# Refitted engine orders, other mask forms and half-bank sums in a top-k attention and MLP-mixer kernel

## The chip, the cores and the metric

The kernel runs on one core of a Trainium2 chip. A core has a matrix engine (TensorE, PE), a vector engine (VectorE, DVE), an activation engine (ScalarE, ACT), a general engine (GpSimd, POOL) and queues that start transfers (SyncE, SP, among them). All run side by side, each takes its own instructions in order, and semaphores join them. The metric is device time in microseconds of one execution, as the median of several; the profile is of one execution.

## The reference

There are 8 batches of 8 heads, 576 rows and 64 columns per head. Each row of scores keeps its 32 largest, and the masked softmax weights the values; then an MLP mixer works on each batch, over the rows (256 hidden) and then over the 512 channels (1536 hidden).

```python
scores = scale * np.matmul(q, k.transpose(0, 1, 3, 2))
kth = np.partition(scores, -32, axis=-1)[..., -32:-31]
scores = np.where(scores >= kth, scores, -1000000000.0)
scores = scores - np.max(scores, axis=-1, keepdims=True)
attn = np.exp(scores); attn = attn / (np.sum(attn, axis=-1, keepdims=True) + 1e-09)
x = np.matmul(attn, v)            # then (B, S, H * D), as x of the mixer
h = np.maximum(x.transpose(0, 2, 1) @ w_tok1, 0.0) @ w_tok2
u = x + h.transpose(0, 2, 1)
out = u + np.maximum(u @ w_ch1, 0.0) @ w_ch2
```

## The kernel before

The kernel is straight-line code, written out by a planner. Each operation is added with its engine, an assumed duration, a due time, the operations it depends on and the buffers it takes and frees. The planner then walks a model of the engines: on each engine, of the operations that could start at the same time, the one with the earliest due time goes first. The result is only an order of instructions for each engine; on the chip they run as semaphores let them. The due times come from the table `W`, in units of `T` after a row's own time, so `W` sets priorities.

```python
W = dict(
    T=2.45, ev=-0.8, evh=0.45, seg=2.15, t2=3.1, ct=1.2, xm=3.65, dm=3.2, m5=3.25, ex=3.95, tn=3.15,
    z=6.0, mk=0.8, pm=3.85, rw=4.55, og=6.55, eg=2.8, ea=1.95, st=4.25, tr=0.35, pv=7.65, fin=8.2,
    mlp=15.75, stp=1.95, mlq=13.3, stq=0.85, hp=7.35, hps=1.55,
)
FORMS = ("DRDAD", "RDADA", "DRDRD", "RDDRA")   # 5 units of a pair of heads; pair p takes FORMS[p % 4]
LAST = ("DRRDR", "QAADA")                      # the last two of the 32 pairs
```

Two heads of a batch form a pair. A pair has five units: four full ones (128 query rows of both heads, so two rows of 128 x 576 scores) and a short one (64 remaining query rows of both heads, in one row). Every unit first goes the same way (shortened):

```python
om  # PE   L413/L405: scores into PSUM ("big": 4 buffers of two banks each)
evs # ACT  L471: copy of the scores to SBUF (S), one per row
# per row:
segs # DVE L478: 8 largest of each of 7 segments of the row
a1..a5 # DVE L481, L482, L489: from these, an upper threshold (thi)
cts # ACT  L492: Sign against the threshold, with a count (sg, cnt)
xm  # POOL L495: X = S * sg, once per unit
dm  # DVE  L503: 9 filler values that fix the rank
m   # DVE  L507: the 8 largest of X; the last is the exact threshold (tlo)
```

Then the masked exponential Pm is made in one of four forms, by the unit's letter:

```python
if form == "D":
    ex   # ACT  L515: E = exp(S)
    tn, zs, mk  # POOL L517, L520, L523: M = 0/1 mask from S and the threshold
    last # POOL L526: Pm = E * M
elif form in ("R", "Q"):
    if form == "R":
        ws # ACT L533: W = relu(tlo - S), one per row
    else:
        tn, zs, ws # POOL L517/540, L542, L546: W = min(S - tlo, 0), scaled
    og   # PE L553 and L413/L405: sink * W into PSUM, then the scores added on top once more
    last # ACT L559: Pm = exp(PSUM), one per row
else:    # "A"
    ex   # ACT L564: exp(S) into PSUM, one per row
    last # DVE L567: Pm = (S >= tlo) * exp, one per row
```

A transposing transfer turns Pm (the last two units of the last pair: PE and a DVE copy, L578 and L582), PE multiplies by the values (L436), and DVE divides by the row sums (L454, L455). After four pairs the mixer of that batch is spread among the next pairs' units; the last batch has nothing to hide behind and has a way of its own. Three of its four column blocks come early, and their part of the hidden sums is put aside in SBUF. When the last block is there, each of the 12 hidden blocks is finished so:

```python
for fc in range(NF):
    pb = Buf("big")
    o = plan.add("PE", 0.28, d, lambda ...: hidden(pb, fc, (NC - 1,)), ...)        # L736, two matmuls of 288 columns
    a = plan.add("DVE", 0.7, d + 0.3, lambda ...: nc.vector.tensor_tensor(         # L784
        out=part(fc), in0=row(pb.t), in1=part(fc), op=ALU.add), [o, ready[fc]], use=[pb, B_])
    relus.append(plan.add("ACT", 0.53, d + 0.6, lambda ...: nc.scalar.activation(  # L786
        out=H2.t[:, fc, :], in_=part(fc), func=AF.Relu), [a], use=[B_, H2]))
    if fc < NF - 2:
        # L768: five output sums of this hidden block, in three "big" buffers that stay taken
        prev = plan.add("PE", 1.09, d + 1.5, f, [relus[-1], prev], use=[H2] + outs)
```

So one "big" buffer of four is left for the sums of this loop.

Of the kernel before, what the change touches and what calls it, by code (L numbers as in the profile page):

```python
# [8 lines left out]
P = 128  # L9
# [7 lines left out]
SINK2 = float(2.0**50)  # L17

W = dict(
    T=2.45, ev=-0.8, evh=0.45, seg=2.15, t2=3.1, ct=1.2, xm=3.65, dm=3.2, m5=3.25, ex=3.95, tn=3.15,  # L20
    z=6.0, mk=0.8, pm=3.85, rw=4.55, og=6.55, eg=2.8, ea=1.95, st=4.25, tr=0.35, pv=7.65, fin=8.2,
    mlp=15.75, stp=1.95, mlq=13.3, stq=0.85, hp=7.35, hps=1.55,
)

FORMS = ("DRDAD", "RDADA", "DRDRD", "RDDRA")

LAST = ("DRRDR", "QAADA")
NEG = -float(2.0**120)
BIG = float(2.0**60)

# [178 lines left out]
def kernel(  # L209
# [11 lines left out]
    nc = tc.nc  # L221
# [3 lines left out]
    AF = mybir.ActivationFunctionType  # L225
# [27 lines left out]
    plan = Plan()  # L253
# [85 lines left out]
    def row(t):  # L339
        return flat(t)[:, L0 : L0 + S]  # L340

    def pair_ops(p):
# [76 lines left out]
        for g in range(5):  # L419
            n = 2 if g < 4 else 1  # L420
            bs, Ss = [Buf("big") for _ in range(n)], Buf("S")
            i0 = 9 * p + 2 * g
            om = plan.add("PE", 1.2 if g < 4 else 1.1, T * i0, lambda g=g, bs=bs: scores(g, bs, True), [eq, ek], acq=bs + [Ss], use=[qT, kT])
            PT.append(unit_ops(i0, n, bs, Ss, om, p, g, scores, [qT, kT]))


# [39 lines left out]
    def unit_ops(i0, n, s, S_, om, p, g, scores, qkT):  # L466
# [7 lines left out]
        for h in range(n):  # L474
# [17 lines left out]
            cts.append(plan.add("ACT", 0.77, th + W["ct"] * T, lambda h=h, i=i, r=r: nc.scalar.activation(  # L492
                out=sg.t[:, h, :], in_=S_.t[:, h, :], func=AF.Sign, scale=-CUT, bias=thi[:, r + 7 : r + 8],
                accum_out=cnt[:, i : i + 1]), [a5], acq=[sg] if h == 0 else [], use=[S_, sg]))
        xm = plan.add("POOL", 0.1 + 1.16 * n, te + W["xm"] * T, lambda: nc.gpsimd.tensor_tensor(  # L495
            out=X.t[:, XW - S : XW - S + n * S].rearrange("p (h c) -> p h c", h=n), in0=S_.t[:, 0:n, :], in1=sg.t[:, 0:n, :], op=ALU.mult),
            cts, acq=[X], use=[S_, sg])
        if not first_x:
# [14 lines left out]
        if form == "D":  # L513
            E, M, Z, nt = Buf("E"), Buf("M"), Buf("Z"), Buf("nt")
            ex = plan.add("ACT", 0.1 + 0.48 * n, te + W["ex"] * T, lambda: nc.scalar.activation(  # L515
                out=E.t[:, 0:n, :], in_=S_.t[:, 0:n, :], func=AF.Exp, scale=scale / UP), evs, acq=[E], use=[S_])
            tn = plan.add("POOL", 0.2, te + W["tn"] * T, lambda: nc.gpsimd.tensor_scalar(  # L517
                out=nt.t[:, 0:n], in0=tlo[:, r0 - n + 1 : r0 + 1], scalar1=-(1.0 - 2.0**-24), scalar2=0.0,
                op0=ALU.mult, op1=ALU.add), ms, acq=[nt])
            zs = [plan.add("POOL", 0.835, te + W["z"] * T + 0.01 * h, lambda h=h: nc.gpsimd.tensor_scalar(  # L520
# [8 lines left out]
        elif form in ("R", "Q"):  # L529

            Wm, es = Buf("M"), [Buf("big") for _ in range(n)]
            if form == "R":
                ws = [plan.add("ACT", 0.68, te + W["rw"] * T + 0.2 * h, lambda h=h: nc.scalar.activation(  # L533
                    out=Wm.t[:, h, :], in_=S_.t[:, h, :], func=AF.Relu, scale=-1.0,
                    bias=tlo[:, r0 - h : r0 - h + 1]), [ms[h]], acq=[Wm] if h == 0 else [], use=[S_, Wm])
                    for h in range(n)]
            else:
                nt, Z = Buf("nt"), Buf("Z")
                tn = plan.add("POOL", 0.2, te + W["tn"] * T, lambda: nc.gpsimd.tensor_scalar(
                    out=nt.t[:, 0:n], in0=tlo[:, r0 - n + 1 : r0 + 1], scalar1=-(1.0 - 2.0**-24), scalar2=0.0,  # L540
                    op0=ALU.mult, op1=ALU.add), ms, acq=[nt])
                zs = [plan.add("POOL", 0.835, te + W["z"] * T + 0.01 * h, lambda h=h: nc.gpsimd.tensor_scalar(  # L542
                    out=Z.t[:, h, :], in0=S_.t[:, h, :], scalar1=nt.t[:, n - 1 - h : n - h],
                    scalar2=16.0, op0=ALU.add, op1=ALU.mult), [tn], acq=[Z] if h == 0 else [],
                    use=[S_, nt, Z]) for h in range(n)]
                ws = [plan.add("POOL", 0.27 + 0.48 * n, te + W["mk"] * T, lambda: nc.gpsimd.tensor_scalar(  # L546
                    out=Wm.t[:, 0:n, :], in0=Z.t[:, 0:n, :], scalar1=0.0, scalar2=-float(2.0**40), op0=ALU.min,
                    op1=ALU.max), zs, acq=[Wm], use=[Z])]

            def again():  # L550
                for h in range(n):
                    for lo, hi in ((0, HS), (HS, S)):
                        nc.tensor.matmul(  # L553
                            out=row(es[h].t)[:, lo:hi], lhsT=sink[:, "RQ".index(form), :], rhs=Wm.t[:, h, lo:hi],
                            start=True, stop=False)
                scores(g, es, False)

            og = plan.add("PE", (1.2 if n == 2 else 1.1) + 0.3 * n, te + W["og"] * T, again, ws, acq=es, use=[Wm] + qkT)
            last = [plan.add("ACT", 0.535, te + W["eg"] * T + 0.2 * h, lambda h=h: nc.scalar.activation(  # L559
                out=Pm.t[:, h, 0:S], in_=row(es[h].t), func=AF.Exp, scale=scale / UP),  # L560
                [og], acq=[Pm] if h == 0 else [], use=[es[h], Pm]) for h in range(n)]
# [31 lines left out]
    def form_of(p, g):  # L593
        if p >= NPAIR - 2:
            return LAST[p - NPAIR + 2][g]
        return FORMS[p % len(FORMS)][g]

    def mlp_ops(b):
        X = xb[b]
# [62 lines left out]
        for fc in range(NF):  # L662
# [7 lines left out]
                            rhs=UT.t[:, cc, lo:hi], start=(cc == 0), stop=(cc == NC - 1))  # L670

            d = due()
            o = plan.add("PE", 1.02, d, f, uts + l3, acq=[pb] + ([H2] if fc == 0 else []), use=[UT, H2])
            h2.append(plan.add("ACT", 0.535, d + 1, lambda fc=fc, pb=pb: nc.scalar.activation(  # L674
                out=H2.t[:, fc, :], in_=row(pb.t), func=AF.Relu), [o], use=[pb, H2]))
        for s0 in (0, 2, 4):
# [5 lines left out]
            for h in range(sn):  # L682
                pb = Buf("one")
                for part in range(2):
                    def f(part=part, sc=s0 + h, pb=pb, r=r):
# [5 lines left out]
                        if part:  # L691
                            for cc in range(NC):
# [2 lines left out]
                                    start=False, stop=(cc == NC - 1))  # L695

                    d = due()
                    o = plan.add("PE", 1.6 if part else 1.33, d, f, dep + l4,
                                 acq=[] if part else [pb], use=[H2, pb] + ([UT] if part else []))
                    dep = [o]  # L700
                es.append(plan.add("ACT", 0.48, d + 1, lambda pb=pb, ob=ob, r=r, h=h: nc.scalar.copy(
# [11 lines left out]
    def mlp_tail(b, base, UT, H2, uts):  # L713
# [16 lines left out]
                return flat(B_.t).bitcast(f32)  # L730
            return B_.t[:, :, :, :].rearrange("p t h d -> p (t h d)")[:, 0:S]

        def hidden(pb, fc, ccs):
            for lo, hi in ((0, HS), (HS, S)):
                for cc in ccs:
                    nc.tensor.matmul(  # L736
                        out=row(pb.t)[:, lo:hi], lhsT=wc1b[:, cc, fc * P : (fc + 1) * P],
                        rhs=UT.t[:, cc, lo:hi], start=(cc == ccs[0]), stop=(cc == ccs[-1]))

        ready = []  # L740
        for fc in range(NF):
# [1 line left out]
            B_, half = parts[fc]  # L743
            d = base - T * W["hp"] + W["hps"] * T * fc
            dep = uts[0 : NC - 1] + l3 + (late_d if B_.tag in ("E", "Z") else [])
            o = plan.add("PE", 0.78, d, lambda fc=fc, pb=pb: hidden(pb, fc, range(NC - 1)), dep,
                         acq=[pb] + ([H2] if fc == 0 else []) + ([B_] if half == 0 else []), use=[UT, H2, B_])
            ready.append(plan.add("ACT", 0.525, d + 0.1, lambda fc=fc, pb=pb: nc.scalar.copy(
                out=part(fc), in_=row(pb.t)), [o], use=[pb, B_, H2]))
# [24 lines left out]
        relus = []  # L774
        prev = None
        for fc in range(NF):
            pb = Buf("big")
            B_, half = parts[fc]
            d += 1.4
            o = plan.add("PE", 0.28, d, lambda fc=fc, pb=pb: hidden(pb, fc, (NC - 1,)), uts + [ready[fc]],  # L780
                         acq=[pb], use=[UT, H2])
            if fc == 0:
                prev = plan.add("PE", 0.4, d + 0.1, lambda: residual((NC - 1,)), uts + [r1], use=[UT] + outs)
            a = plan.add("DVE", 0.7, d + 0.3, lambda fc=fc, pb=pb: nc.vector.tensor_tensor(  # L784
                out=part(fc), in0=row(pb.t), in1=part(fc), op=ALU.add), [o, ready[fc]], use=[pb, B_])
# [269 lines left out]
```

## Time and profile before

| what | value |
|---|---|
| time, median of three | 857.64 us (857.32 to 860.5) |
| span of the profiled execution | 858.9 us |
| instructions | 19498 |
| mean granted TensorE clock | 0.92 |
| HBM read, written | 35.85 MB, 9.44 MB |
| score matmuls L413 | 1400, 250.0 us busy |
| POOL product X L495 | 160, 344.7 us busy |
| DVE segment maxima L478 | 2016, 403.4 us busy |

The profile gives for every engine the time in which at least one of its instructions was running. Instructions of one engine overlap a little, so durations of single ones add up to more than the busy time of their group. PE is TensorE's matmul, PEld its weight load. A group line names the kernel's line, the engine, the operation, what it writes and reads, how often it ran, its busy time, the mean duration in ns, and the idle time of the engine just before it with what ended it. The clock is the share of TensorE's full rate that was granted in a stretch.

### The profile page before, as it was taken

How to read it: one execution, taken by the hardware profiler on the slowest of the kernel's cores; microseconds unless marked ns; L12 is line 12 of the kernel's file. 1: busy time of each engine (PE TensorE's matmuls, PEld its weight loads, DVE VectorE, ACT ScalarE, POOL GpSimd, SP SyncE). 2: the span in 40 equal slices, each digit the busy share in tenths (PEclk: the TensorE clock that was granted, in tenths of full speed). 3: DMA queues.
4: the chain of work that ended last, by engine and by line, in shares of the span. 5: the costliest groups of instructions: out<-in, count | busy, mean ns of one | idle time of the engine just before them, and what ended most of it. 6: DMA issues, size and time to landing. Idle time of an engine off the chain costs nothing.

```text
span 858.9 us, 19498 instructions
## 1 busy us (share of the span) xinstructions
PE 698.7 (81%) x5458; PEld 445.9 (52%) x5495; DVE 795.4 (93%) x4783; ACT 766.4 (89%) x1465; POOL 723.4 (84%) x557
## 2 busy tenths in 40 slices
PE   6756648898788898899688886888888886899984
PEld 4434425655456555565356554564555554575641
DVE  5999899998999999999999999999999999999852
ACT  6997778998999989999999999999899999999742
POOL 2999988899889998899998998899898999889600
PEclk9675688998999899999899998999899998999998
DMA  5985866436555446446565355746557345343401
GB/s 125 152 160 95 123 119 115 100 65 119 125 100 112 86 115 136 82 100 120 124 121 106 76 123 109 124 84 124 115 109 129 70 109 128 67 71 67 105 2 60
DMA packets 311061, 89.58 MB, mean 104 GB/s; under 512 B 303776, under 2 KB 305696, under 8 KB 310944
## 3 DMA queue, kind: packets, MB, share of 16 engines
q1 hardware_dynamic: 306992, 84.19, 49.8%
q0 software_dynamic: 2752, 3.77, 3.2%
q8 instruction: 45, 0.74, 0.4%
q14 instruction: 72, 0.59, 0.2%
q10 hardware_dynamic: 1200, 0.30, 0.2%
HBM read 35.85 MB, written 9.44 MB: 53 GB/s over the span
## 4 chain that ended last, share of the span: by engine, by line
DVE 42%; ACT 23%; PE 20%; issue 6%; POOL 5%; DMA 3%; SPq 1%; ACTq 0%; DVEq 0%; POOLq 0%
DVE cd L478 15%; DVE tlo L507 11%; ACT sg L492 8%; PE big L413 6%; PE big L688 6%; ACT S L471 5%; DVE cd L482 5%; DVE Pm L567 3%; DVE m L481 3%; ACT M L533 2%; ACT Pm L559 2%; POOL X L495 2%; DVE thi L489 2%; DVE X L503 2%; PE big L768 2%
## 5 line engine op out<-in xcount | busy, mean ns | idle before, releaser
L478 DVE MAX8 cd<-S 128x8 f32<-128x82 f32 (+1 forms) x2016 | 403.4, 230 | 18.0 <-ACT S L471 17.9
L495 POOL TENSOR_TENSOR X<-S,sg 128x1152 f32<-128x1152 f32 (+1 forms) x160 | 344.7, 2167 | 51.4 <-ACT sg L492 42.0
L413 PE MATMUL big<-kT,qT 64*128 64x288 f32 x1400 | 250.0, 478 | 45.5 <-ACT kT L394 31.8
L492 ACT ACTIVATE sg<-S,thi 128x576 bf16<-128x576 f32 x288 | 227.1, 790 | 13.2 <-POOL X L495 4.8
L507 DVE MAX8 tlo<-X 128x8 f32<-128x588 f32 x288 | 220.4, 765 | 3.0 <-POOL X L495 1.6
L413 PEld LDWEIGHTS big<-kT,qT 64*128 64x128 f32 x1400 | 151.6, 214 | 106.6 <-ACT kT L394 34.5
L471 ACT COPY S<-big 128x576 f32<-128x576 f32 x288 | 174.5, 651 | 9.3 <-PE big L413 8.8
L526 POOL TENSOR_TENSOR Pm<-E,M 128x1152 bf16<-128x1152 bf16 (+1 forms) x78 | 168.3, 2157 | 6.5
L520 POOL TENSOR_SCALAR Z<-S,nt 128x576 f32<-128x576 f32 x141 | 105.0, 745 | 13.5
L688 PE MATMUL big<-wc2b,H 128*128 128x512 bf16 (+1 forms) x401 | 99.7, 387 | 13.2 <-ACT S L471 5.9
L668 PE MATMUL big<-UT,wc1b 128*128 128x288 bf16 x672 | 91.2, 286 | 13.7 <-ACT H L674 5.4
L481 DVE MAX8 m<-cd 128x8 f32<-128x14 f32 (+1 forms) x576 | 97.4, 170 | 0.3
L482 DVE MATCH_REPLACE8 cd<-m,cd 128x14 f32<-128x14 f32 (+1 forms) x576 | 97.4, 169 | 0.0
L523 POOL TENSOR_SCALAR M<-Z 128x1152 bf16<-128x1152 f32 (+1 forms) x78 | 82.2, 1054 | 6.8
L515 ACT ACTIVATE E<-S 128x1152 bf16<-128x1152 f32 (+1 forms) x78 | 84.7, 1086 | 2.7 <-POOL Pm L526 0.8
L668 PEld LDWEIGHTS <-wc1b 128*128 128x128 bf16 x672 | 64.1, 97 | 40.0 <-issue 23.5
L553 PE MATMUL big<-M,sink 128*128 128x288 bf16 x190 | 39.4, 313 | 43.6 <-ACT M L533 27.8
L688 PEld LDWEIGHTS <-H 128*128 128x128 bf16 (+1 forms) x420 | 40.6, 101 | 61.7 <-issue 24.9
L559 ACT ACTIVATE Pm<-big 128x576 bf16<-128x576 f32 x95 | 56.7, 654 | 16.9 <-PE big L413 16.9
L533 ACT ACTIVATE M<-S,tlo 128x576 bf16<-128x576 f32 x93 | 69.7, 783 | 2.2 <-DVE tlo L507 2.0
L436 PEld LDWEIGHTS <-PT 128*128 128x128 bf16 x1600 | 54.9, 100 | 15.2 <-issue 7.1
L436 PE MATMUL big<-vb,PT 128*128 128x65 bf16 x1600 | 57.1, 197 | 5.8 <-DMA PT<-Pm 5.1
(109 smaller groups left out, 914.3 us busy)
## 6 DMA issues: line engine op xcount, KB each, us to landing
qL<-in_q_dram SPq DMA_DIRECT2D x64, 128.0 KB, 2.9
vL<-in_v_dram SPq DMA_DIRECT2D x64, 128.0 KB, 2.9
kL<-in_k_dram SPq DMA_DIRECT2D x62, 128.0 KB, 2.8
out_dram<-ob SPq DMA_DIRECT2D x14, 512.0 KB, 3.0
PT<-Pm SPq DMA_TRANSPOSE x158, 3.5
wc1b<-in_moe_w_ch_dram POOLq DMA_DIRECT2D x4, 384.0 KB, 6.0
wc2b<-in_moe_w_ch_dram POOLq DMA_DIRECT2D x4, 384.0 KB, 6.1
qL<-in_q_dram SPq DMA_DIRECT2D x64, 16.0 KB, 2.3
```

The costliest lines, as they stand in the source:

```text
L413: nc.tensor.matmul(out=row(bs[h].t)[:, lo:hi], lhsT=qT.t[r, g * P : (g + 1) * P], rhs=kT.t[r, lo:hi], start=start, stop=True,)
L436: nc.tensor.matmul(out=o[:, g, :], lhsT=src[:, (5 * h if g < 4 else 0) + j, :], rhs=vb.t[:, j, h, :], start=(j == 0), stop=(j == 4),)
L471: evs = [plan.add("ACT", 0.525, t + W["ev"] * T + W["evh"] * h * T, lambda h=h: nc.scalar.copy(out=S_.t[:, h, :], in_=row(s[h].t)), [om], ...
L478: segs = [plan.add("DVE", 0.148, th + W["seg"] * T + 0.01 * a, lambda a=a, cd=cd, h=h: nc.vector.max(cd.t[:, a, :], S_.t[:, h, bounds[a] : ...
L481: m_ = lambda n_, cd=cd, m8=m8: (lambda: nc.vector.max(m8.t[:, :], cd.t[:, :, 0:n_]))
L482: c_ = lambda n_, cd=cd, m8=m8: (lambda: nc.vector.match_replace(cd.t[:, :, 0:n_], m8.t[:, :], cd.t[:, :, 0:n_], NEG))
L492: cts.append(plan.add("ACT", 0.77, th + W["ct"] * T, lambda h=h, i=i, r=r: nc.scalar.activation(out=sg.t[:, h, :], in_=S_.t[:, h, :], func ...
L495: xm = plan.add("POOL", 0.1 + 1.16 * n, te + W["xm"] * T, lambda: nc.gpsimd.tensor_tensor(out=X.t[:, XW - S : XW - S + n * S].rearrange("p ...
L507: m = plan.add("DVE", 0.682, te + W["m5"] * T + 0.3 * h * T, lambda h=h, r=r: nc.vector.max(tlo[:, r : r + 8], X.t[:, h * XW : (h + 1) * X ...
L526: last = [plan.add("POOL", 0.12 + 1.11 * n, te + W["pm"] * T, lambda: nc.gpsimd.tensor_tensor(out=Pm.t[:, 0:n, 0:S], in0=E.t[:, 0:n, :], i ...
L668: nc.tensor.matmul(out=row(pb.t)[:, lo:hi], lhsT=wc1b[:, cc, fc * P : (fc + 1) * P], rhs=UT.t[:, cc, lo:hi], start=(cc == 0), stop=(cc == ...
L688: nc.tensor.matmul(out=pb.t[0:r, pb.half, :], lhsT=H2.t[:, fc, cs], rhs=wc2b[:, fc, :], start=(fc == 0), stop=False)
```

## The change

Four things change, and nothing of what is computed.

1. `W` is refitted, with a model of the TensorE clock behind the fit, and the assumed durations of PE's and POOL's operations are raised slightly. This changes the order of the instructions on each engine.
2. The first four pairs get their own forms (`FIRST`): no mixer runs beside them, so the engines are loaded otherwise there.
3. The forms of the other pairs (`FORMS`, `LAST`) are chosen anew.
4. In the last batch, each of the 12 inner sums is made in two halves of 288 columns, each in a bank of its own ("one" is half of a "big" buffer), so that PE can fill one half while DVE adds the other.

```diff
 W = dict(
-    T=2.45, ev=-0.8, evh=0.45, seg=2.15, t2=3.1, ct=1.2, xm=3.65, dm=3.2, m5=3.25, ex=3.95, tn=3.15,
-    z=6.0, mk=0.8, pm=3.85, rw=4.55, og=6.55, eg=2.8, ea=1.95, st=4.25, tr=0.35, pv=7.65, fin=8.2,
-    mlp=15.75, stp=1.95, mlq=13.3, stq=0.85, hp=7.35, hps=1.55,
+    T=2.1, ev=-7.1, evh=5.45, seg=10.8, t2=3.2, ct=2.3, xm=3.05, dm=3.5, m5=-3.85, ex=9.2, tn=-1.5,
+    z=5.3, mk=-1.2, pm=-2.7, rw=-3.9, og=7.85, eg=7.95, ea=3.15, st=7.0, tr=-0.45, pv=7.5, fin=-9.5,
+    mlp=11.1, stp=1.35, mlq=13.6, stq=1.2, hp=2.85, hps=5.15,
 )
-FORMS = ("DRDAD", "RDADA", "DRDRD", "RDDRA")
-LAST = ("DRRDR", "QAADA")
+FORMS = ("DRADR", "QQADR", "DRQDD", "RQADR")
+FIRST = ("QRDRD", "RQRQR", "QQRRQ", "DRRQR")
+LAST = ("DQADA", "AAAAD")
 ...
-        return FORMS[p % len(FORMS)][g]
+        return FIRST[p][g] if p < 4 else FORMS[p % len(FORMS)][g]
 ...   (assumed durations, for example)
-            om = plan.add("PE", 1.2 if g < 4 else 1.1, ...
+            om = plan.add("PE", 1.3 if g < 4 else 1.2, ...
-        xm = plan.add("POOL", 0.1 + 1.16 * n, ...
+        xm = plan.add("POOL", 0.1 + 1.19 * n, ...
-            og = plan.add("PE", (1.2 if n == 2 else 1.1) + 0.3 * n, ...
+            og = plan.add("PE", (1.3 if n == 2 else 1.2) + 0.34 * n, ...
 ...   (the last batch)
-            pb = Buf("big")
-            o = plan.add("PE", 0.28, d, lambda fc=fc, pb=pb: hidden(pb, fc, (NC - 1,)), uts + [ready[fc]],
-                         acq=[pb], use=[UT, H2])
+            adds = []
+            for u in range(2):
+                pb = Buf("one")
+                us = slice(u * HS, u * HS + HS)
+                o = plan.add("PE", 0.16, d + 0.4 * u, lambda fc=fc, pb=pb, us=us: hidden(
+                    pb.t[:, pb.half, 0:HS], fc, (NC - 1,), ((us.start, us.stop),)), uts + [ready[fc]],
+                    acq=[pb], use=[UT, H2])
+                adds.append(plan.add("DVE", 0.42, d + 0.3 + 0.4 * u, lambda fc=fc, pb=pb, us=us: nc.vector.tensor_tensor(
+                    out=part(fc)[:, us], in0=pb.t[:, pb.half, 0:HS], in1=part(fc)[:, us], op=ALU.add),
+                    [o, ready[fc]], use=[pb, B_]))
-            a = plan.add("DVE", 0.7, d + 0.3, lambda fc=fc, pb=pb: nc.vector.tensor_tensor(
-                out=part(fc), in0=row(pb.t), in1=part(fc), op=ALU.add), [o, ready[fc]], use=[pb, B_])
-            relus.append(plan.add("ACT", 0.53, d + 0.6, lambda fc=fc: nc.scalar.activation(
-                out=H2.t[:, fc, :], in_=part(fc), func=AF.Relu), [a], use=[B_, H2]))
+            relus.append(plan.add("ACT", 0.57, d + 1.2, lambda fc=fc: nc.scalar.activation(
+                out=H2.t[:, fc, :], in_=part(fc), func=AF.Relu), adds, use=[B_, H2]))
```

More of the change, by code (lines that the diff above doesn't have):

```diff
@@ L422, in pair_ops @@
             i0 = 9 * p + 2 * g
-            om = plan.add("PE", 1.2 if g < 4 else 1.1, T * i0, lambda g=g, bs=bs: scores(g, bs, True), [eq, ek], acq=bs + [Ss], use=[qT, kT])
+            om = plan.add("PE", 1.3 if g < 4 else 1.2, T * i0, lambda g=g, bs=bs: scores(g, bs, True), [eq, ek], acq=bs + [Ss], use=[qT, kT])
             PT.append(unit_ops(i0, n, bs, Ss, om, p, g, scores, [qT, kT]))
@@ L494, in unit_ops @@
                 accum_out=cnt[:, i : i + 1]), [a5], acq=[sg] if h == 0 else [], use=[S_, sg]))
-        xm = plan.add("POOL", 0.1 + 1.16 * n, te + W["xm"] * T, lambda: nc.gpsimd.tensor_tensor(
+        xm = plan.add("POOL", 0.1 + 1.19 * n, te + W["xm"] * T, lambda: nc.gpsimd.tensor_tensor(
             out=X.t[:, XW - S : XW - S + n * S].rearrange("p (h c) -> p h c", h=n), in0=S_.t[:, 0:n, :], in1=sg.t[:, 0:n, :], op=ALU.mult),
@@ L516, in unit_ops @@
                 out=E.t[:, 0:n, :], in_=S_.t[:, 0:n, :], func=AF.Exp, scale=scale / UP), evs, acq=[E], use=[S_])
-            tn = plan.add("POOL", 0.2, te + W["tn"] * T, lambda: nc.gpsimd.tensor_scalar(
+            tn = plan.add("POOL", 0.29, te + W["tn"] * T, lambda: nc.gpsimd.tensor_scalar(
                 out=nt.t[:, 0:n], in0=tlo[:, r0 - n + 1 : r0 + 1], scalar1=-(1.0 - 2.0**-24), scalar2=0.0,
@@ L538, in unit_ops @@
                 nt, Z = Buf("nt"), Buf("Z")
-                tn = plan.add("POOL", 0.2, te + W["tn"] * T, lambda: nc.gpsimd.tensor_scalar(
+                tn = plan.add("POOL", 0.29, te + W["tn"] * T, lambda: nc.gpsimd.tensor_scalar(
                     out=nt.t[:, 0:n], in0=tlo[:, r0 - n + 1 : r0 + 1], scalar1=-(1.0 - 2.0**-24), scalar2=0.0,
@@ L556, in again @@
                 scores(g, es, False)
-            og = plan.add("PE", (1.2 if n == 2 else 1.1) + 0.3 * n, te + W["og"] * T, again, ws, acq=es, use=[Wm] + qkT)
+            og = plan.add("PE", (1.3 if n == 2 else 1.2) + 0.34 * n, te + W["og"] * T, again, ws, acq=es, use=[Wm] + qkT)
             last = [plan.add("ACT", 0.535, te + W["eg"] * T + 0.2 * h, lambda h=h: nc.scalar.activation(
@@ L672, in mlp_ops @@
             d = due()
-            o = plan.add("PE", 1.02, d, f, uts + l3, acq=[pb] + ([H2] if fc == 0 else []), use=[UT, H2])
+            o = plan.add("PE", 1.06, d, f, uts + l3, acq=[pb] + ([H2] if fc == 0 else []), use=[UT, H2])
             h2.append(plan.add("ACT", 0.535, d + 1, lambda fc=fc, pb=pb: nc.scalar.activation(
@@ L697, in mlp_ops @@
                     d = due()
-                    o = plan.add("PE", 1.6 if part else 1.33, d, f, dep + l4,
+                    o = plan.add("PE", 1.68 if part else 1.4, d, f, dep + l4,
                                  acq=[] if part else [pb], use=[H2, pb] + ([UT] if part else []))
@@ L731, in part, with hidden @@
             return B_.t[:, :, :, :].rearrange("p t h d -> p (t h d)")[:, 0:S]
-        def hidden(pb, fc, ccs):
-            for lo, hi in ((0, HS), (HS, S)):
+        def hidden(dst, fc, ccs, cols=((0, HS), (HS, S))):
+            for lo, hi in cols:
                 for cc in ccs:
                     nc.tensor.matmul(
-                        out=row(pb.t)[:, lo:hi], lhsT=wc1b[:, cc, fc * P : (fc + 1) * P],
+                        out=dst[:, lo - cols[0][0] : hi - cols[0][0]], lhsT=wc1b[:, cc, fc * P : (fc + 1) * P],
                         rhs=UT.t[:, cc, lo:hi], start=(cc == ccs[0]), stop=(cc == ccs[-1]))
@@ L745, in mlp_tail @@
             dep = uts[0 : NC - 1] + l3 + (late_d if B_.tag in ("E", "Z") else [])
-            o = plan.add("PE", 0.78, d, lambda fc=fc, pb=pb: hidden(pb, fc, range(NC - 1)), dep,
+            o = plan.add("PE", 0.8, d, lambda fc=fc, pb=pb: hidden(row(pb.t), fc, range(NC - 1)), dep,
                          acq=[pb] + ([H2] if fc == 0 else []) + ([B_] if half == 0 else []), use=[UT, H2, B_])
@@ L776, in mlp_tail @@
         for fc in range(NF):
-            pb = Buf("big")
             B_, half = parts[fc]
             d += 1.4
-            o = plan.add("PE", 0.28, d, lambda fc=fc, pb=pb: hidden(pb, fc, (NC - 1,)), uts + [ready[fc]],
-                         acq=[pb], use=[UT, H2])
-            if fc == 0:
-                prev = plan.add("PE", 0.4, d + 0.1, lambda: residual((NC - 1,)), uts + [r1], use=[UT] + outs)
-            a = plan.add("DVE", 0.7, d + 0.3, lambda fc=fc, pb=pb: nc.vector.tensor_tensor(
-                out=part(fc), in0=row(pb.t), in1=part(fc), op=ALU.add), [o, ready[fc]], use=[pb, B_])
-            relus.append(plan.add("ACT", 0.53, d + 0.6, lambda fc=fc: nc.scalar.activation(
-                out=H2.t[:, fc, :], in_=part(fc), func=AF.Relu), [a], use=[B_, H2]))
+            adds = []
[8 more added lines that the diff above has]
+                    [o, ready[fc]], use=[pb, B_]))
+            if fc == 0:
+                prev = plan.add("PE", 0.4, d + 0.5, lambda: residual((NC - 1,)), uts + [r1], use=[UT] + outs)
+            relus.append(plan.add("ACT", 0.57, d + 1.2, lambda fc=fc: nc.scalar.activation(
+                out=H2.t[:, fc, :], in_=part(fc), func=AF.Relu), adds, use=[B_, H2]))
             if fc < NF - 2:
@@ L791, in f @@
                         outer(t, fc)
-                prev = plan.add("PE", 1.09, d + 1.5, f, [relus[-1], prev], use=[H2] + outs)
+                prev = plan.add("PE", 1.12, d + 2.0, f, [relus[-1], prev], use=[H2] + outs)
         for t in range(5):
@@ L797, in f @@
                     outer(t, fc)
-            prev = plan.add("PE", 0.44, d + 2 + 0.1 * t, f, [prev] + relus[NF - 2 :], use=[H2] + outs)
+            prev = plan.add("PE", 0.45, d + 2.5 + 0.1 * t, f, [prev] + relus[NF - 2 :], use=[H2] + outs)
             ob = obs[t // 2]
             eng = nc.vector.tensor_copy if t % 2 == 0 else nc.scalar.copy
-            e = plan.add("DVE" if t % 2 == 0 else "ACT", 0.6, d + 3, lambda t=t, ob=ob, eng=eng: eng(
+            e = plan.add("DVE" if t % 2 == 0 else "ACT", 0.6, d + 3.5, lambda t=t, ob=ob, eng=eng: eng(
                 out=ob.t[0 : rows[t], t % 2, 0:C], in_=acc(t, 0, C)), [prev],
```

## Prediction

> **What bounds the kernel now.** I read the busy times first, then a table of stages with granted clock, then the chain of work that ended last, then the waits of each stage, and last the tail instruction by instruction.
>
> ```profile
> PE 698.7 (81%) x5458; PEld 445.9 (52%) x5495; DVE 795.4 (93%) x4783; ACT 766.4 (89%) x1465; POOL 723.4 (84%) x557
> ...
> DVE 42%; ACT 23%; PE 20%; issue 6%; POOL 5%; DMA 3%; SPq 1%; ACTq 0%; DVEq 0%; POOLq 0%
> ```
>
> VectorE (DVE) is busy 795.4 of 858.9 us, so all that a new order of the same work can recover is its 63.5 us of idleness. The table of stages says where that lies. Its columns are the stretch, its length, busy time of each engine, granted TensorE clock, DMA share and GB/s.
>
> ```profile
> 0.00:16.00 16.00, 10.32 (x48) 7.38 (x48) 5.86 (x60) 7.83 (x11) 0.70 (x6) 1.00 0.58 129
> 16.00:118.00 102.00, 64.08 (x388) 40.94 (x388) 97.24 (x614) 84.65 (x164) 95.49 (x79) 0.70 0.79 131
> 118.00:805.00 687.00, 584.42 (x4728) 376.30 (x4760) 667.88 (x4055) 651.18 (x1255) 618.41 (x466) 0.95 0.53 105
> 805.00:826.00 21.00, 19.72 (x209) 14.27 (x210) 12.22 (x38) 12.94 (x24) 8.81 (x7) 1.00 0.12 23
> 826.00:846.00 20.00, 17.59 (x80) 6.20 (x81) 10.03 (x16) 8.09 (x13) 0.00 (x0) 1.00 0.00 1
> 846.00:859.00 13.00, 2.61 (x12) 0.81 (x10) 2.14 (x4) 1.69 (x3) 0.00 (x0) 0.70 0.29 98
> ```
>
> DVE's idle time, length less busy, is by stage: start 10.1, the first four pairs 4.8, the body 19.1, the end of the last pair 8.8, the last batch's inner sums 10.0, the last stores 10.9; together 63.7 (the stages run to 859.0). In the body DVE is at 97%, ScalarE (ACT) at 95%, GpSimd (POOL) at 90%, TensorE (PE) at 85%: four engines near their limit, with DVE just ahead. In the first four pairs POOL is at 94% beside DVE's 95%, and PE at only 63% with a clock of 0.70. In three neighbouring stretches of that stage PE looks like this (stretch, length, PE busy, clock, DMA, GB/s):
>
> ```profile
> 57.80:61.20 3.40, 2.53 (x18) 1.00 1.10 230
> 61.20:64.60 3.40, 0.00 (x0) 0.71 0.78 151
> 64.60:68.00 3.40, 1.77 (x6) 0.50 0.84 134
> ```
>
> After a stretch with no matmul the clock is a half, and PE works at that half when work returns.
>
> [...]the score matmul (L413) takes 402 ns at the shortest and 847 at the longest. [...]I take DVE's 93% as it stands, and PE's 85% only as a sign of how much room there may be. [...] No run here has yet shown the halved add. [...]
>
> **The change, part by part. The forms.** After the second maximum, a unit (128 query rows of two heads, or the short unit of one row tile) makes its masked exponentials in one of four forms. I count units from the form strings, 128 full and 32 short. Before: D 63 full and 15 short, R 46 and 1, A 18 and 16, Q 1 and 0. After (first four pairs by FIRST, 26 pairs by FORMS, two by LAST): D 43 and 8, R 27 and 22, A 25 and 1, Q 33 and 1. The costs are means from the groups by shape:
>
> ```profile
> L526 POOL TENSOR_TENSOR Pm<-E,M 128x1152 bf16<-128x1152 bf16 x63 | 149.1, 2367 | 5.2
> L520 POOL TENSOR_SCALAR Z<-S,nt 128x576 f32<-128x576 f32 x141 | 105.0, 745 | 13.5
> L515 ACT ACTIVATE E<-S 128x1152 bf16<-128x1152 f32 x63 | 74.2, 1177 | 2.5 <-POOL Pm L526 0.8
> L523 POOL TENSOR_SCALAR M<-Z 128x1152 bf16<-128x1152 f32 x63 | 72.2, 1146 | 5.5
> L533 ACT ACTIVATE M<-S,tlo 128x576 bf16<-128x576 f32 x93 | 69.7, 783 | 2.2 <-DVE tlo L507 2.0
> L559 ACT ACTIVATE Pm<-big 128x576 bf16<-128x576 f32 x95 | 56.7, 654 | 16.9 <-PE big L413 16.9
> ```
>
> - POOL: 20 full D products fewer x 2.367 = -47.3; 7 short x 1.275 = -8.9; Z rows 143 -> 161 x 0.745 = +13.4; M 12 full more x 1.146 and 6 short fewer x 0.666 = +9.8; nt +1. Sum **-32 us**, 723 -> 691.
> - ACT: E 20 full fewer x 1.177 and 7 short x 0.699 = -28.4; relu rows 93 -> 76 x 0.783 = -13.3; second exponential rows 95 -> 143 x 0.654 = +31.4; A rows 52 -> 51, -0.7. Sum **-11 us**, 766 -> 755.
> - DVE: A rows 52 -> 51 x 0.804 = -0.8. Nothing.
> - PE: 48 more rows (R and Q) that form their scores a second time. In the timeline four sink matmuls took 0.65 us and the eight score matmuls of a full unit 1.25 (clock 0.94 in that stretch), less some 0.2 that overlaps: 1.7 for two rows, so 48 x 0.85 = **+41 us**, 699 -> 740 at today's clock.
>
> So no work leaves the engine that bounds; POOL and ACT, the two behind it, get room, and PE pays.
>
> **The first four pairs.** D falls from 8 full and 2 short units to 2 and 1, Q rises from 0 to 6 and 1. POOL there, before: 16 x 2.388 + 4 x 1.286 for X = 43.4; D 8 x 5.19 + 2 x 2.88 = 47.3; weight loads 8.4; together 99, against 95.5 seen. After: 43.4 + 10.4 + 2.9 + Q 6 x 2.83 + 1.6 + 8.4 = 84. DVE loses six A rows there (4.8 us), which come back later. R and Q rows rise from 12 to 31: 19 x 0.85 = 16 us of PE at full clock, up to twice that at half clock, on 64 busy of 102; the pauses fill, so more of it should run at full clock. So POOL stops being the second bound and DVE alone holds the stage. I give it 2.5 of its 4.8 us of idleness.
>
> **The body.** Of POOL's 32 us, 17 fall here (15 in the first pairs), and they are no gain by themselves; the gain is what DVE idles less. Its waits there are few: 6.9 us for the output matmuls ahead of the reciprocal (L454), 6.3 for score copies by ACT, about a microsecond each for POOL and for A's exponentials. The refitted order puts the first-stage maxima late (seg 2.15 -> 10.8) and the closing maxima early (m5 3.25 -> -3.85), with score copies early (ev -0.8 -> -7.1): work that releases other engines goes first, and the 2016 small maxima fill the gaps. That is the right direction for the copy waits. Against it, PE takes 41 - 16 = 25 us more in 687, from 85% to 89%, and the waits for PE may grow. I choose 4 us less idleness of 19.
>
> **The tail.** Before, one (128 x 576) sum per step sits in the one free PSUM buffer: PE L736 -> DVE L784 0.76 -> ACT L786 0.68 -> PE L768.
>
> ```profile
> 831.80 1.37 PE big L768 x5
> 833.17 0.35 PE big L736 x2
> 833.52 1.20 PE big L768 x5
> 834.72 0.35 PE big L736 x2
> 835.09 1.37 PE big L768 x5
> ```
>
> In this part of the chain two steps take 835.09 - 831.80 = 3.29 us, 1.64 each. From the mean of one L768, 0.381, five in 1.37 are spaced (1.37 - 0.381)/4 = 0.25, and the two L736 by 0.42 - 0.287 = 0.13; PE alone would need 5 x 0.25 + 2 x 0.13 = 1.51. Halves let PE start on the next sum while DVE adds the other half, but the step can't fall below PE's 1.51: 12 x 0.13 = 1.6 us. [...] Ahead of it, the transposes of the last unit stood 3.8 us behind hidden-layer matmuls (the copy L582 waits 3.81 for PE from 814.9), and the chain there is PE without a break. The last pair's forms become AAAAD and hp, hps and fin move that early work; I give this 2 us of the 8.8.
>
> **Sum.** 2.5 + 4 + 1.6 + 2 = 10.1 less, and nothing for the start (loads, then the first score copy, untouched) or the last stores. 857.6 - 10 = **848 us**.
>
> **Rivals.** First, PE becomes the bound. For it: 41 us more, on an engine already at 85% in the body, in order, with a clock that falls to a half after a pause; R, Q and A also need a PSUM buffer twice, and rows that do rise from 147 to 194 for four double-bank buffers. Against it: all DVE waits on PE in the body are some 7 us, and the D units that left need no second buffer. If DVE's waits for scores and for the output matmuls trebled, the body would lose 25 us and the time be about 870. Second, the gain is hidden: POOL and ACT were never the bound, DVE's 97% is what an order can reach, and only the tail moves: 854. Third, the early maxima starve nothing and the body's idleness halves along with a shorter tail: 19 -> 9, so 6 more than I give, 842; with the first pairs at 1 us idle, 840. That is about the floor: 797 DVE busy plus 10 start, 27 tail and a few microseconds between.
>
> **Range and chances.** The sum is small because every part draws on the 63.7 us of idleness, of which start and stores hold 21. Faster by over 2% means under 840.5, the third rival whole: 0.14. Slower by over 2% means above 874.8, the first rival and more: 0.06. The rest, 0.80, is within 2%. The order is the least certain part, since every wait moves: 837 to 862.
>
> **What would show it.** POOL near 691, ACT 755, DVE 796 to 797 and PE about 740 busy confirm the counts; a granted clock above 0.70 in the first four pairs and POOL clearly below DVE there confirm that part. DVE's idleness in the body below 19 shows the order right; more of it, behind L413 or L436, shows the first rival. Steps of 1.5 us between L768 groups show the tail right; 1.64 show that PE, not the buffer, held it. The prediction is wrong if the body's idleness moves by more than 8 us either way.

## The result and the profile after

The changed kernel takes 832.96 us (median of four, 831.03 to 834.18) against 857.48 us (855.79 to 860.5): the ratio is **0.9708, 95% interval 0.9675 to 0.9742**. The prediction was 848, with 837 to 862 as its range; the gain, 24.5 us, is two and a half times the 10 that it said.

The busy times and the chain's shares by engine on the page after:

```profile
PE 735.4 (89%) x5744; PEld 464.6 (56%) x5783; DVE 787.7 (95%) x4794; ACT 753.1 (91%) x1468; POOL 691.4 (83%) x560
...
DVE 73%; PE 10%; ACT 8%; issue 4%; POOL 2%; DMA 1%; SPq 0%; DVEq 0%; ACTq 0%; POOLq 0%
```

POOL, ACT and PE stand within 5 us of the predicted 691, 755 and 740, so the counting of the forms was right. DVE should have stayed near 797 and fell to 787.7. In the chain, DVE's share rose from 42 to 73%: the work that ended last now runs on DVE for most of its length, where before it changed engine again and again.

The table of stages after, with the same columns as before (stretch, length, busy PE, PEld, DVE, ACT, POOL, clock, DMA share, GB/s):

```profile
0.00:16.00 16.00, 10.29 (x51) 7.40 (x51) 5.92 (x61) 7.92 (x14) 0.70 (x6) 1.00 0.57 129
16.00:118.00 102.00, 75.89 (x542) 48.61 (x541) 101.22 (x656) 95.68 (x191) 90.18 (x80) 0.90 0.81 142
118.00:785.00 667.00, 617.32 (x4953) 393.57 (x4990) 661.83 (x4035) 634.25 (x1244) 597.86 (x473) 0.99 0.54 108
785.00:818.00 33.00, 29.41 (x192) 14.23 (x193) 16.66 (x43) 13.67 (x22) 2.63 (x3) 0.95 0.00 1
818.00:831.00 13.00, 2.46 (x10) 0.74 (x9) 2.08 (x4) 1.61 (x3) 0.00 (x0) 0.71 0.29 98
```

DVE's idleness is now 10.1 us at the start (as before), 0.8 in the stretch of the first pairs (4.8), 5.2 in the body (19.1), and 27.3 in the tail (29.7). That is 20.3 us less, and with 7.7 us less busy time it makes, to within 0.2, the 28.2 us between the spans. In the body DVE is at 99.2%.

Here are DVE's longest waits; a line gives the waiting line, what it waited for, the sum in us, how often, and the longest. First before, then after:

```profile
DVE cd L478 <- ACT S L471: 17.9, 17, 9.0
DVE rd L454 <- PE big L436: 10.6, 11, 2.4
DVE PT L582 <- PE big L578: 4.4, 2, 3.8
```

```profile
DVE cd L479 <- ACT S L472: 8.9, 1, 8.9
DVE qL L787 <- PE big L737: 3.3, 2, 2.3
DVE vL L787 <- PE big L737: 2.7, 3, 1.3
```

Of the 17.9 us for score copies, 9.0 are the first copy of the run, which stays; the other sixteen waits are gone, and so are most of those of L454 for the output matmuls (1.2 us left). What is left on top of the list lies in the last loop.

### The profile page after: what moved, and what is told of

It is laid out like the page before. It is cut to its first block, busy times and chain, and to the rows that moved or that the text cites. A ratio compares the mean times of both kernels' runs of the same rounds, so it can differ in the third digit from the quotient of the medians.

```text
span 830.7 us, 20132 instructions
## 1 busy us (share of the span) xinstructions
PE 735.4 (89%) x5744; PEld 464.6 (56%) x5783; DVE 787.7 (95%) x4794; ACT 753.1 (91%) x1468; POOL 691.4 (83%) x560
## 4 chain that ended last, share of the span: by engine, by line
DVE 73%; PE 10%; ACT 8%; issue 4%; POOL 2%; DMA 1%; SPq 0%; DVEq 0%; ACTq 0%; POOLq 0%
DVE cd L479 28%; DVE tlo L508 18%; DVE cd L483 9%; DVE m L482 5%; DVE X L504 3%; DVE thi L490 3%; PE big L414 3%; DVE Pm L568 3%; DVE Xb L456 2%; ACT S L472 2%; ACT sg L493 2%; PE big L769 1%; PE big L624 1%; POOL X L496 1%; PE big L737 1%
## 5 line engine op out<-in xcount | busy, mean ns | idle before, releaser
L414 PE MATMUL big<-kT,qT 64*128 64x288 f32 x1504 | 255.4, 439 | 13.0 <-ACT kT L395 11.5
L493 ACT ACTIVATE sg<-S,thi 128x576 bf16<-128x576 f32 x288 | 232.0, 807 | 16.6 <-DVE thi L490 12.0
L527 POOL TENSOR_TENSOR Pm<-E,M 128x1152 bf16<-128x1152 bf16 (+1 forms) x51 | 112.1, 2198 | 4.3
L669 PE MATMUL big<-UT,wc1b 128*128 128x288 bf16 x672 | 95.1, 286 | 19.7 <-ACT Pm L560 7.7
L560 ACT ACTIVATE Pm<-big 128x576 bf16<-128x576 f32 x143 | 88.4, 674 | 6.8 <-PE big L414 4.8
L521 POOL TENSOR_SCALAR Z<-S,nt 128x576 f32<-128x576 f32 x94 | 70.3, 748 | 8.8
L554 PE MATMUL big<-M,sink 128*128 128x288 bf16 x286 | 53.5, 293 | 18.8 <-ACT M L534 5.6
L406 PE MATMUL big<-kT,qT 128*128 128x288 f32 x220 | 66.8, 427 | 3.7 <-ACT S L472 1.4
L493 ACT ACTIVATION_READ_ACCUMULATOR sg<-S,thi 128x1 f32 x288 | 64.9, 225 | 0.0
L534 ACT ACTIVATE M<-S,tlo 128x576 bf16<-128x576 f32 x76 | 56.4, 784 | 2.7 <-DVE tlo L508 2.4
```

The costliest lines, as they stand in the source:

```text
L414: nc.tensor.matmul(out=row(bs[h].t)[:, lo:hi], lhsT=qT.t[r, g * P : (g + 1) * P], rhs=kT.t[r, lo:hi], start=start, stop=True,)
L527: last = [plan.add("POOL", 0.12 + 1.11 * n, te + W["pm"] * T, lambda: nc.gpsimd.tensor_tensor(out=Pm.t[:, 0:n, 0:S], in0=E.t[:, 0:n, :], i ...
L669: nc.tensor.matmul(out=row(pb.t)[:, lo:hi], lhsT=wc1b[:, cc, fc * P : (fc + 1) * P], rhs=UT.t[:, cc, lo:hi], start=(cc == 0), stop=(cc == ...
```

## The experiments

Each was timed in one session with the kernel before, on the same chip. Three parts of the change can be set apart: the **forms** (F), the **due times** W, and the raised **assumed durations** (D); the fourth is the last loop in halves. I started from two theories: the order made the gain, or the forms did, by the room they give POOL and ACT and the warmer TensorE; a third had the due times pay only with the forms they were fitted to.

### Each part alone, and the last loop

```diff
 # e_b_newW: the kernel before with
-W = dict(T=2.45, ev=-0.8, ..., hps=1.55)
+W = dict(T=2.1, ev=-7.1, ..., hps=5.15)
```

> The kernel before with the refitted due times alone: its forms, its assumed durations and its whole-width last loop stay. Theory 1 (the order made the gain: releasing work first, segment maxima as filler): most of the 28 us comes, 833 to 842, and VectorE's idleness in the body falls from 19 us towards 6. Theory 2 (the forms made it, by the room they give POOL and ACT and the warmer TensorE): little, 850 to 860. Theory 3 (the due times are fitted to their forms and help only with them): no gain or a loss, above 857.

Measured: 865.35 us, ratio 1.0083 (1.0052 to 1.0113): slower. The due times that the prediction called "the right direction" lose time on the old forms. The first theory falls in this shape.

```diff
 # e_b_newforms: the kernel before with
+FORMS = ("DRADR", "QQADR", "DRQDD", "RQADR")
+FIRST = ("QRDRD", "RQRQR", "QQRRQ", "DRRQR")
+LAST = ("DQADA", "AAAAD")
```

> The kernel before with the new forms alone (first four pairs, the others and the last two), old due times and durations. Theory 1: little or a loss, 855 to 870, as 41 us more TensorE work meet the old order. Theory 2: 833 to 845, POOL busy near 691 and the clock of the first four pairs well above 0.70. Theory 3: no gain, above 857.

Measured: 853.14 us, ratio 0.9933 (0.9916 to 0.9950). POOL is busy 691.6 us and the mean clock is 0.974, as in the changed kernel (691.4 and 0.977), and yet only a quarter of the gain is there. Room and a warm TensorE are not enough either. The third theory comes nearest: it had the loss of the due times right, but no gain from the forms where there is a little.

```diff
 # e_oldtail: the changed kernel with the last loop as before
-            for u in range(2):   # two halves of 288 columns, two adds
+            pb = Buf("big")      # one sum of 576 columns, one add
```

> The changed kernel with the last batch's inner sums in whole width again (one PSUM buffer of two banks, one add of 576 columns), all else as changed. The prediction's working says the halves save 1.6 us, so 834.5. The rival, from the trace after (37.2 us from the last UT copy to the end, 33.1 before): the halves cost more than they save, so 829 to 832.

Measured: **828.56 us, ratio 0.9666 (0.9637 to 0.9696)**: the loop in whole width is the faster one, by 4.4 us between the medians; 3.2 us of it lie in the tail (43.7 us from the start of the last exact threshold, as against 46.9). The rival was right. By its median this is the fastest kernel of all that ran, and most later experiments start from it.

```diff
 # e_nofirst: the changed kernel with
-FIRST = ("QRDRD", "RQRQR", "QQRRQ", "DRRQR")
+FIRST = FORMS
```

> The changed kernel with the general forms in the first four pairs too, in place of their own. If the first pairs' own forms give what the prediction put there, some 2.5 us slower, 835.5; if they are the larger part of the gain (VectorE idle there fell from 4.8 to 0.8 us), 837 to 842; if they do nothing, 833.

Measured: 844.53 us, ratio 0.9854 (0.9823 to 0.9884), 11.6 us slower than the changed kernel. Part of it is plain work: the general forms put six A rows into these pairs (57 instead of 51 in the groups), 6 x 0.805 = 4.8 us of DVE. The rest came with another order; which waits make it was not followed up.

### Clock, room and filler

```diff
 # f_b_fill: the kernel before; f_newW_fill: e_b_newW; in full D units
+            for h in range(2):   # second half of the scores once more
+                nc.tensor.matmul(out=row(bs[h].t)[:, HS:S], ...)
```

> The kernel before, and in each of the 63 full units of form D the second half of the score matmuls is issued once more (the same values written again): about 35 us more TensorE work at full clock, nothing else. Clock theory (with the old forms TensorE pauses long enough to fall to half rate, and its late results make the waits; work that fills the pauses cures it): faster than before, 845 to 853, clock 0.96 or more. Room theory (the new forms help by the 32 us taken off POOL and 11 off ACT): slower than before by a few us, 858 to 866, whatever the clock does.

> The kernel before with the refitted due times and the same filler of TensorE work. Without the filler the refitted due times lost 0.8% on the old forms (865). Clock theory: now they gain, 838 to 850. Room theory: 860 to 870, since POOL and ACT have as much to do as before.

Measured: 871.17 us, ratio 1.0164 (1.0100 to 1.0229), and 878.61 us, ratio 1.0245 (1.0199 to 1.0291). The clock was 0.938 and 0.929, where the kernel before had 0.921 to 0.938 in the same session: the filler did not raise it, and the runs show what TensorE work costs and not what a warm clock brings. e_b_newforms says a little more, though with other forms: clock 0.974, gain 0.7%.

```diff
 # f_ot_pool: e_oldtail, full D units
-            zs = [... Z row h ...]
+            zs = [... Z row h, and row 0 computed twice ...]
```

> The changed kernel with the last loop in whole width (828.6), and in each of the 43 full D units the first Z row computed twice on POOL: 43 x 0.748 = 32 us, so POOL has as much work as before the change, in the same order. Room theory: 840 to 850. Clock theory: POOL at 88% still waits for others, 829 to 833.

Measured: 858.23 us, ratio 1.0001 (0.9984 to 1.0019): 30 us for 32 us of POOL work, on an engine that was at 84%. The whole gain is gone, and the waits of DVE say how:

```profile
DVE tlo L508 <- POOL X L496: 25.1, 43, 0.8
```

There are 43 waits, as many as repeated rows, and the longest is about a row's length (0.748 us). In the changed kernel this line sums to 0.3 us. In the order of e_oldtail half of the X products end less than 0.3 us before the maximum that reads them starts (the changed kernel's median is 0.27), so a row of 0.748 us more in front of them is seen by DVE at once, although POOL idles elsewhere.

```diff
 # f_ot_seg: e_oldtail with
-    seg=10.8
+    seg=2.15
```

> The changed kernel with the last loop in whole width, and the due time of the segment maxima as before the change (seg 2.15 for 10.8), so that they no longer stand behind all other work of VectorE. If segment maxima as filler are what lets VectorE run without gaps: 838 or more, with idleness in the body near 10 us. If this one time doesn't matter: 827 to 832.

Measured: 845.78 us, ratio 0.9864 (0.9819 to 0.9908), 17 us slower than e_oldtail. The idleness of DVE from 142 to 730 us, though, is 588 - 583.72 = 4.3 us against 1.9, not the 10 expected. Of the 17.3 us between the two spans, 8.1 lie behind the start of the last exact threshold (843.0 - 791.2 = 51.8 us against 43.7), and the rest is spread over busy time and idleness ahead of it. At that point I took it for the effect of this one due time on the segment maxima; the last experiments make that doubtful.

### Room or fit

```diff
 # g_pool_planned: f_ot_pool, and the planner is told
-            plan.add("POOL", 0.835, ...
+            plan.add("POOL", 0.835 + (0.748 if n == 2 and h == 0 else 0), ...
 # h_b_lesspool: the kernel before, full D units: Z for half the columns
-                out=Z.t[:, h, :], in0=S_.t[:, h, :], ...
+                out=Z.t[:, h, 0:HS], in0=S_.t[:, h, 0:HS], ...
```

> The 32 us of repeated POOL rows again (in the changed kernel with the last loop in whole width), but now the planner is told: the repeated row counts 0.748 us more, and all orders are planned anew around it. Theory of room (POOL's 32 us are worth that time themselves): still 850 to 860. Theory of fit (the repeated rows hurt because the fixed orders did not expect them): most comes back, 830 to 840.

> The kernel before with POOL relieved and nothing else: in the full D units the Z rows are computed for 288 of 576 columns only (the rest of Z stays as it was; the masks of these columns are left out of the computation), orders and all other work as before. POOL falls by some 126 x 0.3 = 40 us. Theory of room: 835 to 848. Theory of fit (only orders fitted to the load pay): 853 to 858.

Measured: 875.58 us, ratio 1.0171 (1.0136 to 1.0205), and 857.85 us, ratio 0.9974 (0.9959 to 0.9988). Telling the planner did not bring the time back; the new order was worse. And 30 us less of POOL work in the old order (693.5 busy; the masks of 288 columns are left out there, and a half row took 0.505 us where I had expected less) gave a quarter of a per cent. So POOL's room is needed by the fitted order and worth almost nothing to the old one. Room alone falls as the cause.

```diff
 # h_nn_olddurs: e_oldtail with all assumed durations as before, for example
-            om = plan.add("PE", 1.3 if g < 4 else 1.2, ...
+            om = plan.add("PE", 1.2 if g < 4 else 1.1, ...
```

> New forms and refitted due times together, but the assumed durations as before the change, and the last loop in whole width: it lacks only the raised durations against the 828.6 us kernel. If the raised durations of TensorE and POOL operations (with which the planner sees nearer the truth) matter: 836 or more. If forms and due times are the whole gain: 827 to 832.

Measured: 848.55 us, ratio 0.9851 (0.9805 to 0.9896). This was the surprise: the raised durations, which the prediction did not weigh at all, make 20 us of difference in this setting.

```diff
 # h_halves_order: the changed kernel; half sums of block fc wait in line
-            ... uts + [ready[fc]],
+            ... uts + [ready[fc]] + (outers[fc - 2 : fc - 1] if fc >= 2 else []),
```

> The changed kernel with its halves, but each half sum of block n follows the output sums of block n-2 on TensorE, so that no half is queued ahead of work that is ready. If the loss of the halves is the order at the loop's start and the clock it drops (0.75 from 798 to 805 us): 829 to 831. If the two adds in place of one cost it: 832 to 834.

Measured: 830.74 us, ratio 0.9658 (0.9626 to 0.9690), within the first expectation; see the tail below.

### All combinations, and a shift of 10 ns

Still open was whether the durations help by being truer. I ran the missing combinations, and PE's and POOL's durations put back apart.

```diff
 # k_b_durs: before with D; k_newW_durs: before with W and D
 # m_oldW_durs: e_oldtail with the old W
 # k_oldPEdurs: e_oldtail with PE's durations as before; k_oldPOOLdurs: with POOL's
```

> The kernel before with the raised assumed durations alone (forms, due times and the whole-width loop as before). Theory of truer times (they help any plan): 838 to 850. Theory of a joint fit (due times, forms and durations only pay together): 853 to 870.

> Old forms with refitted due times and raised durations, whole-width loop: it lacks only the forms against the 828.6 us kernel. If due times and durations together are the gain: 830 to 840. Theory of a joint fit: above 853, as the due times were fitted to other forms.

> The 828.6 us kernel with TensorE's assumed durations put back (score matmuls 1.2 for 1.3, second scores, mixer matmuls), POOL's left raised. If TensorE's durations carry the 20 us: 842 to 850. If POOL's do: 828 to 833. Theory of a joint fit, in which any shift of the assumptions scrambles the order: both runs slow, 838 to 850.

> The 828.6 us kernel with POOL's assumed durations put back (X product 2.42 for 2.48 per full unit, negated thresholds 0.2 for 0.29), TensorE's left raised. If POOL's durations carry the 20 us: 842 to 850. If TensorE's do: 828 to 833. Theory of a joint fit: both runs slow, 838 to 850.

> New forms and raised durations with the old due times, whole-width loop: the last of the combinations. New forms with old due times and old durations took 853. If truer durations help the new forms by themselves: 840 to 848. If all three only pay as fitted together: 850 to 860.

All combinations, with the loop in whole width (the ratio is to the kernel before in the same session):

| forms | due times | durations | median us | ratio (95%) |
|---|---|---|---|---|
| old | old | old | 857.48 | 1 |
| old | new | old | 865.35 | 1.0083 (1.0052 to 1.0113) |
| old | old | new | 868.82 | 1.0108 (1.0062 to 1.0154) |
| old | new | new | 862.37 | 1.0043 (1.0022 to 1.0063) |
| new | old | old | 853.14 | 0.9933 (0.9916 to 0.9950) |
| new | old | new | 853.23 | 0.9916 (0.9885 to 0.9947) |
| new | new | old | 848.55 | 0.9851 (0.9805 to 0.9896) |
| new | new | PE's old | 846.86 | 0.9844 (0.9800 to 0.9888) |
| new | new | POOL's old | 844.80 | 0.9847 (0.9800 to 0.9895) |
| new | new | new | 828.56 | 0.9666 (0.9637 to 0.9696) |

The raised durations do not help by themselves (868.82), nor with the new forms (853.23); PE's and POOL's put back alone cost about the same. So the three parts pay most of their gain together, as a joint fit would. POOL's raised values are not the truer ones either: the X product of a full unit takes 2.381 us on average in the changed kernel, and the assumption went from 2.42 to 2.48; the negated thresholds take 0.193, and it went from 0.20 to 0.29. The last experiment shifts one assumption by an amount that can hardly matter by its meaning:

```diff
 # m_om131: e_oldtail with
-            om = plan.add("PE", 1.3 if g < 4 else 1.2, ...
+            om = plan.add("PE", 1.31 if g < 4 else 1.2, ...
```

> The 828.6 us kernel with one assumed duration shifted by 10 ns (full score matmuls 1.31 us for 1.30), all else as it is. If the durations matter by their meaning: nothing, 827 to 831. If the gain is one order picked out of many by the fit, and any shift lands on another: 838 to 850, like the runs with older durations.

Measured: 840.35 us, ratio 0.9784 (0.9738 to 0.9830). Ten nanoseconds in one assumption cost 11.8 us, with the same instructions on every engine. Where they are lost can be read. Of the 12.7 us between the two spans, 5.1 lie ahead of the start of the last exact threshold (787.1 against 782.0 us; from 142 to 730 us DVE is busy 584.11 of 588 against 586.05). The other 7.6 lie behind it: 838.4 - 787.1 = 51.3 us against 825.7 - 782.0 = 43.7. Three of DVE's adds in the last loop wait long for PE there:

```profile
818.10 0.76 DVE L785 TENSOR_TENSOR Z<-big,Z 128x576 f32<-128x576 f32 x1 [3.59 <-PE big L737]
821.46 0.76 DVE L785 TENSOR_TENSOR Z<-big,Z 128x576 f32<-128x576 f32 x1 [2.60 <-PE big L737]
824.41 0.76 DVE L785 TENSOR_TENSOR kT<-big,kT 128x576 f32<-128x576 f32 x1 [2.19 <-PE big L737]
```

In the fitted order these three waits are 0.72, 1.05 and 0.79 us. In the shifted one the early sums of these blocks come only inside the loop (ACT puts them aside from 816.9 us on), where the fitted order had them all done before it. f_ot_seg has the same fault, with four blocks.

With the older durations the loss lies elsewhere: ahead of the last exact threshold, which starts 15 to 22 us later than in the fitted order (801.8 us with all of them put back, 803.5 with PE's, 797.1 with POOL's), while the part behind it is only 0.8 to 2.4 us longer. So the shift shows that the fitted order is one that a trifle can spoil, above all in its tail. It does not show that the 20 us of the durations are such a trifle too.

## Why the prediction was wrong

The sum was 2.5 for the first pairs, 4 for the body and 3.6 for the tail, and nothing for DVE's busy time. By the tables of stages, DVE's idleness fell by 4.0, 13.9 and 2.4 us, and its busy time by 7.7. So two steps failed most: the 4 us for the body, and busy time as a floor.

**The counts: right.** 48 more rows that form their scores twice were to cost 41 us of PE and PE's busy time rose by 36.7; POOL's and ACT's sums came to within 2 us. Two of the groups behind it (line, engine, operation, shapes, count, busy us and mean ns):

```profile
L527 POOL TENSOR_TENSOR Pm<-E,M 128x1152 bf16<-128x1152 bf16 x43 | 101.9, 2369 | 3.6
...
L560 ACT ACTIVATE Pm<-big 128x576 bf16<-128x576 f32 x143 | 88.4, 674 | 6.8 <-PE big L414 4.8 <-ACT sg L493 0.9 <-PE big L406 0.7
```

**"About the floor: 797 DVE busy": wrong.** I took busy time for work. Where DVE did not idle between two instructions, they overlapped by some 0.08 us (from 16 to 780 us the median is 0.082 before and 0.083 after), as here after the change (start, length):

```profile
301.33 0.16 DVE L482 MAX8 m<-cd 128x8 f32<-128x14 f32 x1
301.41 0.23 DVE L479 MAX8 cd<-S 128x8 f32<-128x83 f32 x1
301.55 0.07 DVE L483 MATCH_VALUE_LOAD cd<-m,cd 128x8 f32 x1
```

The second starts 0.08 us before the first ends, the third 0.09 before the second. An instruction in front of which DVE idles has no such overlap. From 16 to 780 us DVE has 114 idle gaps before and 53 after. As an estimate, 61 x 0.083 = 5.1 us of busy time, against a fall of 7.7 with about 1 us of work added. The rest has no account here.

**"I choose 4 us less idleness of 19" in the body: mis-sized.** It fell by 13.9. The mechanism was named: copies early, closing maxima early, segment maxima as filler. Those due times alone lose time on the old forms, so what they mean for DVE isn't enough. What the runs show in its place: every order with the new forms and no work added beat the one before, none of the three other orders with the old forms did, and which order the planner lands on with the new forms is worth 12 to 25 us more (828.56 against 840.35 to 853.23). My third rival had 9 us of idleness left in the body and called 840 the floor; nothing in the profile supported a floor that far above DVE's own work.

**"They are no gain by themselves", of POOL's 17 us in the body: half right.** Less POOL in the old order gives 0.26%; the same POOL work put back into the fitted order takes all. POOL was busy for 84% of the time there, and the order had no slack for 32 us more.

**The first four pairs, 2.5 of 4.8: too small.** DVE idles 0.8 us there and POOL has fallen behind it, 90.2 against 101.2, with the clock at 0.90 for 0.70. That was the predicted sign, though POOL was to be at 84. The six A rows that the stage loses I had expected back in later pairs; the count of A rows over the kernel says so (51 for 52), and without FIRST it is 57. So the first pairs' own forms are worth more than their stage shows: they keep the total of A rows where it was, which is 4.8 of the 11.6 us that e_nofirst lost.

**The tail, 1.6 and 2: wrong in sum.** From the start of the last exact threshold to the end it is 46.9 us in both kernels (858.9 - 812.0 and 830.7 - 783.8). The early part came as predicted and larger: the last UT copy starts 9.7 us after that threshold where it was 13.8. The loop gave it all back. In the steady part two steps take 808.26 - 804.84 = 3.42 us where they took 3.29:

```profile
804.84 1.37 PE L769 MATMUL big<-wc2b,H 128*128 128x512 bf16 x5
...
806.15 0.42 PE L737 MATMUL big<-UT,wc1b 128*128 128x288 bf16 x2
...
806.40 1.36 PE L769 MATMUL big<-wc2b,H 128*128 128x512 bf16 x5
...
806.60 0.82 DVE L787 TENSOR_TENSOR vL<-big,vL 128x288 f32<-128x288 f32 x2 [1.04 <-PE big L737]
...
807.70 0.42 PE L737 MATMUL big<-UT,wc1b 128*128 128x288 bf16 x2
...
808.26 1.37 PE L769 MATMUL big<-wc2b,H 128*128 128x512 bf16 x5
```

The failing step is "halves let PE start on the next sum while DVE adds the other half". In PE's fixed order both halves stand together (x2) behind the five output matmuls, so there is no overlap of a half's matmul with the other half's add; what remains is two adds in 0.82 us where one took 0.76. And at the loop's start, halves were queued ahead of output sums that were ready; PE worked 1.67 of 3 us, and then lost its clock, which is 0.50 from 800 to 802 us (three stretches, columns as in the table of stages):

```profile
795.00:798.00 3.00, 1.67 (x12) 0.92 (x11) 1.49 (x5) 0.68 (x1) 0.00 (x0) 1.00 0.02 5
798.00:801.00 3.00, 2.64 (x9) 0.94 (x9) 1.28 (x4) 0.74 (x2) 0.00 (x0) 0.75 0.00 0
801.00:805.00 4.00, 3.81 (x13) 1.17 (x13) 1.08 (x3) 1.31 (x2) 0.00 (x0) 0.76 0.00 0
```

With the halves lined up behind the output sums (h_halves_order) the clock stays at 1.00 in these stretches, the first two of them below, and the tail takes 827.2 - 782.4 = 44.8 us; in whole width it takes 43.7:

```profile
795.00:798.00 3.00, 2.15 (x10) 0.90 (x10) 1.28 (x6) 1.36 (x2) 0.00 (x0) 1.00 0.00 0
798.00:801.00 3.00, 2.87 (x12) 0.94 (x12) 1.64 (x4) 1.22 (x2) 0.00 (x0) 1.00 0.00 0
```

So of the 3.2 us that the halves cost in the tail, 2.1 are that order and its clock and 1.1 what is left of the halves, by one execution of each; the ratios of the two kernels, 0.9658 and 0.9666, do not tell them apart. The fall came after a stretch in which PE was at 56% (1.67 of 3 us) and not idle; with 72% in the same stretch (2.15 of 3 us, h_halves_order) the clock did not fall. The halved add takes 452 to 456 ns in the groups, where the whole one took 754 to 758 before.

**Open.** Why the older durations cost 15 to 22 us ahead of the tail is not settled, as the orders differ everywhere there. Only one neighbour of the fitted order was run, so how often a shift of this size lands as low as 828.56 is not known. The due times were never fitted anew for the old forms, so a good order for these isn't ruled out. Whether a warm clock is worth anything by itself in the old order wasn't tested, as the filler did not raise it.

## What to carry to other kernels

Where several engines are near full and their orders are fixed ahead of time, busy shares tell what an order may reach, and not what a given one will: leave room in the range for an order that is better by some per cent than its parts suggest. Before a due time or a duration is credited with the gain, test a neighbour (one assumption shifted by 10 ns), and read in which stage it loses. Undo each part of a mixed change: the half-bank loop here cost 4.4 us that the fit's gain hid. Splitting a buffer in two gave no overlap here, because the planned order of its producer, PE, held both halves side by side: look at that order before counting on it.

## What the hardware showed that I had not expected

DVE's busy time for nearly the same work went from 795.4 to 787.7 us, about 5 us of it, as an estimate from 61 idle gaps fewer and the 0.08 us by which two instructions overlap where no gap is between them. And 43 more POOL rows of 0.748 us, 32 us on an engine at 84%, made the kernel 30 us slower.
